# Denominators of the first token group of a linear-attention pair: a 0/1 matmul replaced by DMAs over partitions

## The chip, the cores and the metric

The kernel runs on one NeuronCore of one Trainium2 chip. The metric is the device time of one execution in microseconds, taken as the median of several runs. A run also leaves a profile: every instruction of every engine with its start and duration, and the DMAs with their landing times. TensorE (PE) does the matmuls, VectorE (DVE) and ScalarE (ACT) the elementwise work, GpSimd (POOL) and SyncE (SP) mostly issue DMAs.

## The reference

Two independent linear-attention blocks A and B, each on its own x (2048 x 640) and weights, and their outputs side by side:

```python
def block(x, wqkv, wo):                     # x 1 x 2048 x 640, H = 32 heads, Dh = 20
    q, k, v = split_heads(x @ wqkv)
    phi = lambda t: jnp.where(t > 0, t + 1, jnp.exp(t)) + 1e-6
    pq, pk = phi(q), phi(k)
    kv  = jnp.einsum("bhsd,bhse->bhde", pk, v)
    z   = jnp.einsum("bhsd->bhd", pk)
    num = jnp.einsum("bhqd,bhde->bhqe", pq, kv)
    den = jnp.einsum("bhqd,bhd->bhq", pq, z)[..., None] + 1e-6
    return merge_heads(num / den) @ wo
out = concatenate([block(A...), block(B...)], axis=-1)
```

## The kernel before, in words

All matmuls work on float32 values that are split into a rounded high part and a low remainder (names ending in h and l): ACT copies the value to the high part, VectorE subtracts it from the value to get the low part, and TensorE does three matmuls (high by high, high by low, low by high) for each product. `split` is that pair of operations; `later(1, ...)` puts the VectorE half one slot later.

There are two stages. The first works through branches A and B in eight token groups of 512 tokens: k is formed, phi(k) taken, its products with x summed into `gacc` (`psg` in PSUM), the column sums of phi(k) accumulated to DRAM by DMA (`zd`), and from these the matrix m = kv times wo is formed per branch (`kvmm`, `mmm`). m's sums and differences (`form_...`, the tiles f, fh, fl and fs) serve a product scheme of seven products instead of eight (`STEPS`, `product`, `combine`), used for k and again for the output.

The second stage goes through the eight token groups u = 0 to 7 (0 to 3 are branch A, 4 to 7 branch B). For each group `qmm` computes q in five chunks c of 128 columns, 15 matmuls each into a bank `psq`; ACT takes exp and relu from it, VectorE mixes them to phi(q) (`qphi`, line 957), and `qacc` adds z times the chunk to the accumulator `acc` (ACT for chunk 0, VectorE line 980 for the others). Group 6 (`EARLY`) is the exception: its q is computed at the very start of the kernel (`first_chunk`, `q7`, tiles w7 and x7, line 1193), stored, and loaded again late.

The columns of q are ordered by d and head, so one row of acc holds the sum over a part of the d's of one head: partition p belongs to head p mod 32, and the denominator of a head is the sum of four rows, 32 partitions apart. Two ways to form that sum stand in the code:

- group 0 only: `split_acc` splits acc into `ac`, `denmm` multiplies it by the 0/1 matrix `same` (entry 1 where two partitions belong to the same head) in two matmuls into `psd` (lines 993 and 994), and `recip` takes the reciprocal of the result, all 128 partitions by 512 columns, in two halves (line 999). `same` is made early from an iota by two VectorE operations (lines 318 and 319).
- groups 1 to 7: `spread` lays each of the four blocks of acc (32 partitions by 512 columns) over all 128 partitions, as one of four quarters of 128 columns of the tile `da` (four DMAs, line 1008); `invert` adds the quarters and takes the reciprocal of the 128 by 128 sums (lines 1014 to 1016); `gather` lays these back on each of the four blocks of `rd` (four DMAs, line 1025).

Then `divide` multiplies phi(q) by the reciprocals, in place, in two halves of 256 tokens (line 1032), `a_split` and `d_sums` with `d_split` form the left operands of the output product (da and ds, high and low parts, index 0 and 1), and `outmm(u)` does the 14 steps of the output product: seven products n = 0 to 6 for each half q of the group. Product 0 reads da 0, products 1 and 2 read ds 0; products 3 and later read da 1, and products 4 and 6 read ds 1.

The order on each engine is the program's. In the first stage it comes from positions: matmul steps are numbered, `job` places the other work at the position of a step plus a shift from the table SHIFT (and often plus fixed amounts behind the job it follows), and everything is sorted. For instance, for chunk k of the EARLY group:

```python
a = job(("ah", k), a, w7_hi, k)
job(("bh", k), a + 0.2, x7_hi, k)
job(("al", k), a + 0.4, w7_lo, k, after=[("ah", k)])
job(("bl", k), a + 0.6, x7_lo, k, after=[("bh", k)])
```

where a is the position of the first step of chunk k - 1 (for k = 4: 14; for k = 3: 8), and `job` adds and returns the shift. In the second stage work hangs on slots: ("q", i, c, k) is the slot behind the three matmuls k of chunk c of the i-th group in order, ("o", u, s) the slot behind step s of group u's output product; `at(slot, f, ...)` appends to a slot, moved by the table AT along the line of slots. The slots of group 0's output product come behind those of group 1's q. So group 0's denominators, division and splits are placed among the q matmuls of group 1. In group 0's old chain, `split_acc` is moved three slots by AT and `d_split` of index 1 too.

DMAs issued on SP go out in program order: an issue that waits for its data holds up all issues behind it. The same holds for the instructions of ACT when a DMA is issued there.

Of the kernel before, what the change touches and what calls it, by code (L numbers as in the profile page):

```python
# [7 lines left out]
F32 = mybir.dt.float32  # L8
BF16 = mybir.dt.bfloat16
F32R = mybir.dt.float32r  # L10
I32 = mybir.dt.int32
# [3 lines left out]
H = 32  # L15
DH = 20
# [10 lines left out]
    ('c5', 9): 1.08, ('counts',): 0.93, ('exp', 0): 1.45, ('exp', 1): 1.74, ('exp', 10): 0.29, ('exp', 11):  # L27
# [21 lines left out]
    23): 1.04, ('mix', 29): 2.2, ('mix', 3): 0.48, ('mix', 4): -0.12, ('mix', 5): -0.61, ('mix', 7): 1.38,  # L49
# [78 lines left out]
    ('a_split', 1, 0): 2, ('a_split', 2, 0): -1, ('a_split', 3, 0): -1, ('a_split', 4, 0): -3, ('a_split', 5,  # L128
    0): -1, ('a_split', 5, 1): -3, ('a_split', 6, 0): 5, ('a_split', 7, 1): -6, ('d_split', 0, 1): 3,
    ('d_split', 1, 1): 5, ('d_split', 2, 0): -4, ('d_split', 6, 1): 3, ('d_sums', 1, 0): 4, ('d_sums', 3, 1): 3,  # L130
    ('d_sums', 5, 0): 1, ('d_sums', 5, 1): 2, ('d_sums', 6, 1): 4, ('divide', 1, 0): 1, ('divide', 2, 0): 1,
    ('divide', 3, 0): 4, ('divide', 5, 0): 1, ('divide', 6, 0): 2, ('early_acc', 1): 6, ('early_acc', 2): 4,
    ('early_acc', 3): 10, ('early_acc', 4): 2, ('form_last', 'm', 1): 5, ('form_load', 0, 1): 3, ('form_load',
    0, 2): 9, ('form_load', 0, 9): 4, ('form_split', 'm', 1, 0): 5, ('form_split', 'm', 1, 1): -4,
    ('form_split', 'm', 1, 2): -3, ('form_split', 'm', 1, 3): -11, ('form_split', 'm', 1, 5): -4, ('form_split',
    'm', 1, 8): 3, ('form_split', 'm', 1, 9): 5, ('form_sums1', 'm', 1, 1): -5, ('gather', 1): 3, ('invert', 3):
# [14 lines left out]
def tile_linear_attn_pair(ctx: ExitStack, tc: tile.TileContext, ins, out: bass.AP):  # L151
# [153 lines left out]

    def counts():
        ij, at = base.tile([P, D], F32, name="ij", tag="kvt", bufs=1), 0
# [1354 lines left out]
```

## Time and profile before

| what | value |
|---|---|
| median of 3 runs | 560.45 us (560.14 to 561.48) |
| profiled execution: its time, its span | 560.23 us, 558.4 us |
| granted TensorE clock, mean | 0.999 |
| busy TensorE (matmul) | 553.5 us, 99% |
| busy TensorE (weight load) | 505.0 us, 90% |
| busy VectorE, ACT, POOL | 448.4, 334.6, 94.7 us |
| DMA | 116.40 MB, mean 208 GB/s |

The span is the time from the first to the last instruction of the profiled execution; the execution's own time is some 2 us longer. Busy times are unions of instruction records; a row of the profile's timeline is the start in us from the beginning of the span, the duration, the engine, the line of the kernel, the operation, the tile written and the tiles read (buffer numbers left out), and in brackets the idle time before it with what ended it. A row of the waits is who waited for whom: total us, times, longest.

### The profile page before, as it was taken

How to read it: one execution, taken by the hardware profiler on the slowest of the kernel's cores; microseconds unless marked ns; L12 is line 12 of the kernel's file. 1: busy time of each engine (PE TensorE's matmuls, PEld its weight loads, DVE VectorE, ACT ScalarE, POOL GpSimd, SP SyncE). 2: the span in 40 equal slices, each digit the busy share in tenths (PEclk: the TensorE clock that was granted, in tenths of full speed). 3: DMA queues.
4: the chain of work that ended last, by engine and by line, in shares of the span. 5: the costliest groups of instructions: out<-in, count | busy, mean ns of one | idle time of the engine just before them, and what ended most of it. 6: DMA issues, size and time to landing. Idle time of an engine off the chain costs nothing.

```text
span 558.4 us, 9225 instructions
## 1 busy us (share of the span) xinstructions
PE 553.5 (99%) x3339; PEld 505.0 (90%) x3339; DVE 448.4 (80%) x754; ACT 334.6 (60%) x607; POOL 94.7 (17%) x159
## 2 busy tenths in 40 slices
PE   9999999999999999999999999999999999999997
PEld 6898998989898999898988889989898898989997
DVE  5999869989648678797876599798888978798861
ACT  5998466775438686666673677364554646453541
POOL 0022112241101221213301120311101220010110
PEclk9999999999999999999999999999999999999999
DMA  9666577997997657697988965573726489533322
GB/s 298 243 192 140 119 215 189 282 249 232 344 329 195 176 138 210 135 280 222 274 272 250 346 223 206 161 257 100 253 82 216 157 271 382 163 120 114 114 94 95
DMA packets 58430, 116.40 MB, mean 208 GB/s; under 512 B 9104, under 2 KB 22160, under 8 KB 58256
## 3 DMA queue, kind: packets, MB, share of 16 engines
q1 hardware_dynamic: 45056, 74.58, 41.2%
q0 software_dynamic: 12784, 40.97, 26.1%
q8 instruction: 26, 0.43, 0.3%
q10 hardware_dynamic: 544, 0.26, 0.2%
q14 instruction: 20, 0.16, 0.1%
HBM read 69.82 MB, written 42.29 MB: 201 GB/s over the span
## 4 chain that ended last, share of the span: by engine, by line
PE 96%; DVE 2%; DMA 1%; issue 0%; SPq 0%; DVEq 0%
PE pa L356 25%; PE pe L356 13%; PE psg L221 8%; PE psg L220 8%; PE psg L222 8%; PE psb L356 8%; PE psq L220 7%; PE psq L222 7%; PE psq L221 7%; PE pskv L768 1%; DMA wst<-in_A_wk 1%; PE psm L220 1%; PE psq L1193 1%; PE psm L222 1%; PE psm L221 1%
## 5 line engine op out<-in xcount | busy, mean ns | idle before, releaser
L220 PE MATMUL psq<-xqh,wqh 128*128 128x512 f32 x175 | 68.4, 391 | 0.0
L222 PE MATMUL psq<-xqh,wql 128*128 128x512 f32 x175 | 68.2, 390 | 0.0
L221 PE MATMUL psq<-xql,wqh 128*128 128x512 f32 x175 | 68.1, 389 | 0.0
L220 PE MATMUL psg<-pkh,xnh 128*128 128x512 f32 x160 | 62.8, 392 | 0.0
L221 PE MATMUL psg<-pkl,xnh 128*128 128x512 f32 x160 | 62.7, 392 | 0.0
L222 PE MATMUL psg<-pkh,xnl 128*128 128x512 f32 x160 | 62.6, 391 | 0.0
L360 ACT ACTIVATE o<-pa 128x320 f32<-128x320 f32 x64 | 28.0, 438 | 54.5 <-PE pa L356 54.5
L360 ACT ACTIVATE ko<-pa 128x320 f32<-128x320 f32 x64 | 27.7, 435 | 39.7 <-PE pa L356 39.0
L568 POOL DMA_DIRECT2D zd<-ek x30 | 26.6, 886 | 119.2 <-DVE ek L560 53.9
L222 PEld LDWEIGHTS psq<-xqh,wql 128*128 128x128 f32 x175 | 32.9, 188 | 7.0
L221 PEld LDWEIGHTS psq<-xql,wqh 128*128 128x128 f32 x175 | 32.9, 188 | 6.6
L220 PEld LDWEIGHTS psq<-xqh,wqh 128*128 128x128 f32 x175 | 32.8, 188 | 6.5
L222 PEld LDWEIGHTS psg<-pkh,xnl 128*128 128x128 f32 x160 | 30.0, 188 | 6.5
L451 ACT ACTIVATE ksh<-sx 128x512 fp32r<-128x512 f32 x32 | 19.9, 633 | 26.3 <-DVE sx L469 26.2
L221 PEld LDWEIGHTS psg<-pkl,xnh 128*128 128x128 f32 x160 | 30.0, 188 | 5.4 <-DVE pkl L576 0.4
L220 PEld LDWEIGHTS psg<-pkh,xnh 128*128 128x128 f32 x160 | 30.1, 188 | 5.2
L560 DVE SCALAR_TENSOR_TENSOR ek<-ek,ko 128x640 f32<-128x640 f32 x32 | 26.3, 820 | 10.0 <-ACT ko L557 10.0
L955 ACT ACTIVATE pq<-psq 128x512 f32<-128x512 f32 x35 | 20.7, 591 | 19.6 <-PE psq L222 19.6
L572 ACT ACTIVATE pkh<-ek,epst 128x640 fp32r<-128x640 f32 x32 | 26.0, 826 | 8.8 <-DVE ek L560 8.6
L614 DVE TENSOR_TENSOR gacc<-psg,gacc 128x512 f32<-128x512 f32 (+2 forms) x42 | 25.6, 627 | 6.9 <-PE psg L222 6.9
L213 ACT ACTIVATE dah<-pq 128x1024 fp32r<-128x1024 f32 (+2 forms) x24 | 17.7, 772 | 21.9 <-DVE pq L1032 21.9
L957 DVE SCALAR_TENSOR_TENSOR pq<-pq,rq 128x512 f32<-128x512 f32 x35 | 24.0, 687 | 8.3 <-ACT rq L956 8.3
(208 smaller groups left out, 1750.7 us busy)
## 6 DMA issues: line engine op xcount, KB each, us to landing
zd<-ek POOLq DMA_DIRECT2D x32, 320.0 KB, 5.1
out<-o POOLq DMA_DIRECT2D x28, 320.0 KB, 3.5
xt<-in_A_xt_tiles SPq DMA_DIRECT2D x16, 320.0 KB, 5.5
xt<-in_B_xt_tiles SPq DMA_DIRECT2D x16, 320.0 KB, 4.1
xn<-in_B_x SPq DMA_DIRECT2D x16, 320.0 KB, 4.9
xqs<-in_A_xt SPq DMA_DIRECT2D x20, 256.0 KB, 6.6
fdmh<-fsh POOLq DMA_DIRECT2D x14, 320.0 KB, 4.0
fdml<-fsl POOLq DMA_DIRECT2D x14, 320.0 KB, 4.6
```

What stands on the lines that cost most here:

```text
L220: nc.tensor.matmul(o, whi, xhi, start=first, stop=False)
L221: nc.tensor.matmul(o, whi, xlo, start=False, stop=False)
L222: nc.tensor.matmul(o, wlo, xhi, start=False, stop=last)
L356: nc.tensor.matmul(o, x, y, start=start and m == r == 0, stop=m == len(terms) - 1 and r == 2, skip_group_check=True)
L360: nc.scalar.activation(x, y, AF.Copy)
L451: nc.scalar.activation(hi, src, AF.Copy)
L560: nc.vector.scalar_tensor_tensor(ek[n], ek[n], 1.0, rk[n], op0=OP.min, op1=OP.add)
L568: nc.gpsimd.dma_start(zacc[b], e, accum_op=OP.add)
L572: nc.scalar.activation(pk[n][0], ek[n], AF.Identity, bias=epst)
L614: nc.vector.tensor_tensor(o, x, o, op=OP.add)
L955: nc.scalar.activation(e, ps, AF.Exp)
L957: nc.vector.scalar_tensor_tensor(e, e, 1.0, r, op0=OP.min, op1=OP.add)
```

## The change

Group 0 gets its denominators like the groups 1 to 7: `spread`, `invert`, `gather`. For group 0 the eight DMAs alternate between the ACT and the SP queue; for the others all stay on SP. `split_acc`, `denmm`, `recip`, the matrix `same` and its part of the iota go. Group 0's d is formed in another order and partly in later slots: both divides in one slot, a_split before d_sums, and d_split of index 1 inside the output product. The transpose and sum of branch B's z move from group 1's q into group 0's output product. Besides that a number of entries of SHIFT, MOVED and AT change, so that jobs of the first stage, loads, splits and the chains of later groups stand in other places.

The diff, with the tables cut to the entries that are spoken of:

```diff
 SHIFT = {
-... ('ah', 4): -1.75 ... ('al', 3): 0.5 ... ('bl', 1): -0.23 ... ('bl', 3): 0.4, ('bl', 4): 3.53 ...
+... ('ah', 4): -0.43 ... ('al', 3): 1.85 ... ('bl', 1): -0.29 ... ('bl', 3): 3.06, ('bl', 4): 2.02 ...
-... ('c2', 1): 1.11 ... ('exp', 0): 1.45 ... ('mix', 5): -0.61 ... ('nl', 2): 11.78 ... ('qe', 2): -1.84 ...
+... ('c2', 1): 1.24 ... ('exp', 0): 1.24 ... ('mix', 5): 9.51 ... ('nl', 2): 13.98 ... ('qe', 2): -2.5 ...
-... ('s2', 2): 0.94 ... ('wf', 0, 1, 'l'): -0.23 ... ('xh', 3, 'A5'): -5.773 ...
+... ('s2', 2): 1.13 ... ('wf', 0, 1, 'l'): -0.42 ... ('xh', 3, 'A5'): -3.95 ...
 AT = {
+... ('a_split', 0, 0): 1 ... ('d_sums', 0, 0): 2 ... ('gather', 0): 1 ... ('spread', 0): -1 ... ('z_store', 1): -1
-... ('d_split', 0, 1): 3 ... ('split_acc', 0): 3 ... ('load_z', 1): 3 ... ('z_out', 1): 4, ('z_turn', 1): 1
+... ('load_z', 1): 9 ... ('d_sums', 1, 1): 6 ... ('d_split', 2, 1): 6 ... ('divide', 2, 0): 5 ...
...
-    same = base.tile([P, P], F32R)
...
-        nc.gpsimd.iota(mask[P], pattern=[[1, P]], base=0, channel_multiplier=-1)
...
-        ij = mask.pop(P)
-        nc.vector.tensor_scalar(ij, ij, H - 1, None, op0=OP.bitwise_and)
-        nc.vector.tensor_scalar(same, ij, 0.0, None, op0=OP.is_equal)
...
-    def split_acc(u): ...
-    def denmm(u): ...
-    def recip(u, h): ...
     def spread(u):
...
-            nc.sync.dma_start(t[0][:, j * P:(j + 1) * P], acc[u][32 * j:32 * (j + 1), :])
+            (nc.sync if u else (nc.scalar, nc.sync)[j % 2]).dma_start(t[0][:, j * P:(j + 1) * P], acc[u][32 * j:32 * (j + 1), :])
     def gather(u):
...
-            nc.sync.dma_start(r[32 * j:32 * (j + 1), :], y[:, 3 * P:])
+            (nc.sync if u else (nc.scalar, nc.sync)[j % 2]).dma_start(r[32 * j:32 * (j + 1), :], y[:, 3 * P:])
     def outmm(u):
...
-            product(n, ps[q], [da[u, i, q] for i in range(2)], [ds[u, i, q] for i in range(2)], right)
+            product(n, ps[q], [da.get((u, i, q)) for i in range(2)], [ds.get((u, i, q)) for i in range(2)], right)
...
-    at(("q", 1, 3, 3), z_turn, 1)
-    at(("q", 1, 4, 2), z_store, 1)
-    at(("q", 2, 0, 0), z_back, 1)
-    at(("q", 2, 2, 0), z_out, 1)
+    at(("o", 0, 5), z_turn, 1)
+    at(("o", 0, 6), z_store, 1)
+    at(("o", 0, 12), z_back, 1)
+    at(("q", 2, 1, 0), z_out, 1)
...
     chain = {
-        0: [(("q", 1, 0, 0), split_acc, 0), (("q", 1, 1, 1), denmm, 0), (("q", 1, 1, 1), recip, 0, 0),
-            (("q", 1, 1, 1), recip, 0, 1), (("q", 1, 1, 2), divide, 0, 0), (("q", 1, 1, 4), divide, 0, 1),
-            (("q", 1, 2, 0), d_sums, 0, 0), (("q", 1, 2, 2), a_split, 0, 0), (("q", 1, 2, 4), d_sums, 0, 1),
-            (("q", 1, 3, 1), d_split, 0, 0), (("q", 1, 3, 4), a_split, 0, 1), (("q", 1, 4, 1), d_split, 0, 1)]}
+        0: [(("q", 1, 0, 1), spread, 0), (("q", 1, 1, 2), invert, 0), (("q", 1, 1, 2), gather, 0),
+            (("q", 1, 2, 2), divide, 0, 0), (("q", 1, 2, 2), divide, 0, 1), (("q", 1, 3, 0), a_split, 0, 0),
+            (("q", 1, 3, 1), d_sums, 0, 0), (("q", 1, 4, 0), d_split, 0, 0), (("q", 1, 4, 0), a_split, 0, 1),
+            (("q", 1, 4, 1), d_sums, 0, 1), (("o", 0, 1), d_split, 0, 1)]}
```

In SHIFT and AT the position of an entry has no meaning; an entry that is not in the table counts as 0.

More of the change, by code (lines that the diff above doesn't have):

```diff
@@ L121 @@
     ('G', 2, 5): 2.0, ('G', 6, 0): 4.0, ('H', 3, 0, 0): 3.5, ('H', 7, 2, 2): 1.5, ('Q', 1, 1): 2, ('Q', 1, 2):
[3 rows of a table removed]
[3 rows of a table added]
 }
 AT = {
[L128 to L136, printed above, removed]
@@ L137 @@
-    -1, ('invert', 4): -1, ('invert', 5): -2, ('invert', 6): -4, ('kv_step', 1, 5): -2, ('load_px', 4): -1,
-    ('load_w', 'm', 1, 2): 4, ('load_w', 'm', 1, 4): -5, ('load_w', 'q', 1, 4): 8, ('load_xraw', 2, 0): 6,
-    ('load_xraw', 2, 3): 2, ('load_xraw', 4, 2): 6, ('load_xraw', 7, 0): -2, ('load_xraw', 7, 1): 2,
-    ('load_xraw', 7, 3): -6, ('load_xraw', 7, 4): 4, ('load_z', 1): 3, ('m_step', 1, 0): 2, ('m_step', 1, 2): 1,
-    ('m_step', 1, 3): 1, ('round_xq', 1, 0): -2, ('round_xq', 2, 1): -3, ('round_xq', 2, 3): -4, ('round_xq', 4,
@@ L142 @@
-    1): -4, ('round_xq', 4, 2): 2, ('round_xq', 5, 1): 1, ('round_xq', 5, 4): -3, ('round_xq', 7, 1): 4,
-    ('round_xq', 7, 4): -3, ('split_acc', 0): 3, ('split_o', 1, 1): -1, ('split_o', 1, 3): -2, ('split_w', 1,
-    0): -3, ('split_w', 1, 2): -7, ('split_w', 1, 4): 1, ('spread', 6): 6, ('z_out', 1): 4, ('z_turn', 1): 1,
+    ('a_split', 0, 0): 1, ('a_split', 1, 0): 2, ('a_split', 2, 0): -1, ('a_split', 3, 0): -1, ('a_split', 4, 0):
+    -3, ('a_split', 4, 1): 4, ('a_split', 5, 0): -1, ('a_split', 5, 1): -3, ('a_split', 6, 0): 5, ('a_split', 7,
@@ new lines @@
+    1): -6, ('d_split', 1, 1): 5, ('d_split', 2, 0): -4, ('d_split', 2, 1): 6, ('d_split', 6, 1): 3, ('d_sums',
+    0, 0): 2, ('d_sums', 1, 0): 4, ('d_sums', 1, 1): 6, ('d_sums', 3, 1): 3, ('d_sums', 4, 0): -4, ('d_sums', 5,
+    0): 1, ('d_sums', 5, 1): 2, ('d_sums', 6, 1): 4, ('divide', 1, 0): 1, ('divide', 2, 0): 5, ('divide', 3, 0):
+    4, ('divide', 5, 0): 1, ('divide', 6, 0): 2, ('early_acc', 1): 6, ('early_acc', 2): 4, ('early_acc', 3): 10,
+    ('early_acc', 4): 2, ('form_last', 'm', 1): 5, ('form_load', 0, 1): 7, ('form_load', 0, 2): 6, ('form_load',
@@ new lines @@
+    0, 6): 3, ('form_load', 0, 7): -2, ('form_load', 0, 8): -4, ('form_load', 0, 9): 5, ('form_split', 'm', 1,
[3 rows of a table added]
+    ('invert', 3): -1, ('invert', 4): -1, ('invert', 5): -2, ('invert', 6): -4, ('kv_step', 1, 5): -2,
+    ('load_px', 4): -1, ('load_w', 'm', 1, 0): -4, ('load_w', 'm', 1, 2): 3, ('load_w', 'm', 1, 4): -5,
+    ('load_w', 'q', 1, 1): -3, ('load_w', 'q', 1, 4): 8, ('load_xraw', 2, 0): 10, ('load_xraw', 2, 1): 2,
+    ('load_xraw', 2, 2): 6, ('load_xraw', 2, 3): 2, ('load_xraw', 3, 4): -2, ('load_xraw', 4, 2): 6,
@@ new lines @@
+    ('load_xraw', 7, 0): -2, ('load_xraw', 7, 1): 2, ('load_xraw', 7, 3): -6, ('load_xraw', 7, 4): 4, ('load_z',
+    1): 9, ('m_step', 1, 0): 2, ('m_step', 1, 2): 1, ('m_step', 1, 3): 1, ('round_xq', 1, 0): -5, ('round_xq',
+    1, 3): 1, ('round_xq', 2, 0): 2, ('round_xq', 2, 1): -3, ('round_xq', 2, 2): 2, ('round_xq', 4, 1): -4,
+    ('round_xq', 4, 2): 2, ('round_xq', 5, 1): 1, ('round_xq', 5, 4): -3, ('round_xq', 7, 1): 4, ('round_xq', 7,
+    4): -3, ('split_o', 1, 1): -1, ('split_o', 1, 2): -6, ('split_o', 1, 3): -5, ('split_w', 1, 0): -3,
@@ L145 @@
+    ('split_w', 1, 2): -7, ('split_w', 1, 4): 1, ('spread', 0): -1, ('spread', 6): 6, ('z_store', 1): -1,
 }
@@ L307, in counts @@
         ij, at = base.tile([P, D], F32, name="ij", tag="kvt", bufs=1), 0
-        for n in (P, 3 * DH, 2 * DH):
-            mask[n] = ij[:, at:at + n].bitcast(I32) if n == P else ij[:, at:at + n]
+        for n in (3 * DH, 2 * DH):
+            mask[n] = ij[:, at:at + n]
             at += n
-        nc.gpsimd.iota(mask[P], pattern=[[1, P]], base=0, channel_multiplier=-1)
         for nh in (3, 2):
@@ L983, in early_acc @@
         qacc(EARLY, c, px[c])
-    def split_acc(u):
-        t = q2[0].tile([P, 2, 512], F32R, name="ac", tag="sr", bufs=2)
-        split(t[:, 0], t[:, 1], acc.pop(u))
-        acc[u] = t
-    def denmm(u):
-        t = acc.pop(u)
-        ps = den.pop(u) if u in den else bank("psd")
-        nc.tensor.matmul(ps, same, t[:, 0], start=True, stop=False)
-        nc.tensor.matmul(ps, same, t[:, 1], start=False, stop=True)
-        den[u] = (ps, q2[0].tile([P, 512], F32, name="rd", tag="rd", bufs=1))
-    def recip(u, h):
-        ps, r = den[u]
-        nc.vector.reciprocal(r[:, h * 256:(h + 1) * 256], ps[:, h * 256:(h + 1) * 256])
     def spread(u):
```

4 lines of the change are left out of this document (2 added, 2 removed), and 27 rows, old and new, of tables (AT, MOVED, SHIFT).

## The prediction

> **What bounds the kernel now.** I read the page's busy shares and slices first, then the chain that ended last, then what TensorE waited for, then the timeline round the two matmuls that go.
>
> ```profile
> span 558.4 us, 9225 instructions
> PE 553.5 (99%) x3339; PEld 505.0 (90%) x3339; DVE 448.4 (80%) x754; ACT 334.6 (60%) x607; POOL 94.7 (17%) x159
> ...
> PE   9999999999999999999999999999999999999997
> ...
> PE 96%; DVE 2%; DMA 1%; issue 0%; SPq 0%; DVEq 0%
> ...
> PE psi L1137 <- PEq L1647: 0.8, 1, 0.8
> PE psq L1193 <- DVE x7l L210: 0.4, 2, 0.2
> PE psq L1231 <- ACT x7h L1217: 0.2, 1, 0.2
> ```
>
> TensorE is busy in 553.5 of 558.4 us, and 96% of the chain is its own instructions. The last three rows are the whole list of its visible waits, 1.4 us in all, and all of them belong to the preparation of the EARLY group at the start. So time moves here in two ways only: TensorE gets less work, or something arrives too late for it. The other engines' loads matter only through the second.
>
> A busy matmul record overlaps its successor, so what a matmul costs must be read from starts, not durations.
>
> ```profile
> 328.15 0.39 PE L222 MATMUL psq<-xqh,wql 128*128 128x512 f32 x1
> 328.37 0.40 PE L993 MATMUL psd<-ac,same 128*128 128x512 f32 x1
> 328.61 0.40 PE L994 MATMUL psd<-ac,same 128*128 128x512 f32 x1
> 328.84 0.40 PE L220 MATMUL psq<-xqh,wqh 128*128 128x512 f32 x1
> ```
>
> Rows are start, duration, engine, line, tiles. Neighbours start 0.22 to 0.24 us apart though each lasts 0.40.
>
> **The change part by part.**
>
> *The two denominator matmuls.* From the first one's start to the start of the matmul behind them, 328.84 - 328.37 = 0.47 us leave a TensorE that has no visible wait there. Ends: 0.44 us (twice the neighbours' shortest spacing, 328.37 - 328.15 = 0.22) and 0.79 us (both durations, as if nothing overlapped). I take 0.47, the starts being what the successor feels. The Trainium skill, page "TensorE: Matmul & The Clock Gate", section "Wait — 56ns, not 53.3ns?", says a warm matmul of 512 columns starts 215.7 ns after the last. By it the pair would be worth an estimated 0.43 us and the sum below 0.04 us smaller; this case's starts, 0.23 to 0.24 us apart, are slightly longer, and they decide.
>
> *A swap at the start.* Among the changed entries of SHIFT are those of chunk 4 of the EARLY group. Position of a job = position of its step plus its shifts. Before: w7_hi sits at 14 - 1.75 = 12.25, so w7_lo at 12.25 + 0.4 + 2.31 = 14.96 and x7_lo at 12.25 + 0.6 + 3.53 = 16.38. After: w7_hi at 14 - 0.43 = 13.57, w7_lo at 13.57 + 0.4 + 2.31 = 16.28, x7_lo at 13.57 + 0.6 + 2.02 = 16.19. VectorE thus does x7l first. For chunk 3 the two move later (10.2 and 10.3 become 11.55 and 12.96), but no other VectorE job lies between 7.78 and 13.66, so that order stays and its wait stays.
>
> ```profile
> 18.38 0.82 DVE L210 TENSOR_TENSOR w7l<-w,w7h 128x640 fp32r<-128x640 f32 x1
> 19.12 0.69 DVE L210 TENSOR_TENSOR x7l<-x,x7h 128x512 fp32r<-128x512 f32 x1
> 19.72 0.42 DVE L469 TENSOR_TENSOR sx<-xt 128x256 f32<-128x256 f32 x1
> ...
> 19.26 0.39 PE L1193 MATMUL psq<-x7h,w7h 128*128 128x512 f32 x1
> 19.86 0.50 PE L1193 MATMUL psq<-x7l,w7h 128*128 128x512 f32 x1 [0.21 <-DVE x7l L210]
> 20.20 0.40 PE L1193 MATMUL psq<-x7h,w7l 128*128 128x512 f32 x1
> ```
>
> x7l (0.60 us to its successor) would run at 18.38 and w7l at 18.98, done at 18.98 + 0.82 = 19.80. The matmul on x7l can start unhindered at 19.26 + 0.23 = 19.49; that on w7l follows w7l's end by 0.05 us (as 19.86 follows 19.12 + 0.69 = 19.81), at 19.85 instead of 20.20. Gain 0.35 us; late next is w7l, by 0.85 - 0.72 = 0.13. Ends: nothing (something downstream eats it) and 0.48 (20.20 - 19.26 less two spacings of 0.23). I take 0.35.
>
> *First group's denominators by DMAs.* Removed: ACT copy and VectorE difference of ac, two reciprocals. Added: four DMAs out (each lays 32 partitions by 512 columns over 128 by 128), two adds and one reciprocal, four DMAs back, half of them issued by ACT. Seven groups already do this, so their rows price it.
>
> ```profile
> L1008 SPq DMA_DIRECT2D da<-acc x28: 594/606/1229, 348.4 to 512.1; - x28
> L1014 DVE TENSOR_TENSOR da<-da x7: 415/416/427, 354.2 to 514.4; 128x256 f32<-128x256 f32 x7
> L1015 DVE TENSOR_TENSOR da<-da x7: 291/293/293, 354.7 to 514.9; 128x128 f32<-128x128 f32 x7
> L1016 DVE RECIPROCAL da<-da x7: 953/953/954, 355.0 to 515.2; 128x128 f32<-128x128 f32 x7
> ...
> DMA to landing us min/median/max: 2.1/2.2/5.5
> ...
> 0.75 0.41 ACTq L1155 DMA_DIRECT2D x<-in_B_xt_tiles  x1
> ...
> 324.53 0.75 DVE L980 SCALAR_TENSOR_TENSOR acc<-pq,z,acc 128x512 f32<-128x512 f32 x1
> 328.33 0.69 DVE L957 SCALAR_TENSOR_TENSOR pq<-pq,rq 128x512 f32<-128x512 f32 x1 [0.38 <-ACT rq L956]
> 329.04 3.37 DVE L999 RECIPROCAL rd<-psd 128x256 f32<-128x256 f32 x2
> 332.33 2.82 DVE L1032 SCALAR_TENSOR_TENSOR pq<-pq,rd 128x1280 f32<-128x1280 f32 x2
> 341.51 1.22 DVE L210 TENSOR_TENSOR dsl<-sr,dsh 128x1024 fp32r<-128x1024 f32 x1
> 342.65 0.84 DVE L699 STREAM_TRANSPOSE zt<-zs 128x640 f32<-128x640 f32 x1
> 343.52 0.82 DVE L701 TENSOR_REDUCE zr<-zt 128x20 f32<-128x640 f32 x1
> ...
> 343.07 1.76 PE pa L356 x12
> 344.84 1.76 PE pe L356 x12
> ```
>
> (The rows of a tile give ns min/median/max; the last two are from the chain, the first group's output product, whose pe part is the first to need dsl.) In before's clock: acc is done at 324.53 + 0.75 = 325.28. ACT and SP issue two DMAs each, 0.41 to 0.61 us apiece; the last starts at 325.95 and lands 2.2 later, 328.2. The program puts invert behind chunk 0's mix and the second m_step's slot; an ACT delayed by its two issues lets that mix end about 329.4, so invert finds its data there and takes 0.42 + 0.29 + 0.95 = 1.66: 331.1. Back: last issue 331.75, landing 333.95. The divides stand in slot (q,1,2,2) behind chunk 1's mix and accumulation, which end about 334.4 (ACT waits for the reciprocal, issues until 332.05, and then needs about 1.0 for chunk 1's exp and relu; the mix and the accumulation take 0.69 and 0.75, starting 0.6 to 0.7 apart): 334.4 to 337.25, against 332.33 to 335.15 now. The order behind them is a_split 0 (its difference done by 339.7), d_sums 0 (341.0), chunk 3's mix and accumulation (342.3), then dsl: 342.3 + 1.2 = 343.5, against 342.73 now. TensorE, 0.47 us earlier, starts the pe part at 344.37 and reads dsl by its third matmul (12 in 1.76, so 0.15 apart), 344.66. So dsl comes later by 0.8 us and still has 1.2 us; dal (needed at 342.9) has 3. These ends are estimates from the rows above; bounds for the stall follow as rivals. I take nothing. d_split 1 moves into the output product, where the first product to read it is step 8 of 14; I estimate about 2 us left there.
>
> *What is queued behind the new waits.* On SP the spread waits for acc at 325.28; behind it stand the last loads of the forms, wanted from the fourth product on, about 348; from 326.6 they have over 20 us. On ACT, behind the spread, stand two copies of wo and chunk 0's exp and relu, about 1 us late; a bank of psq is wanted again only four allocations on. Behind the gather stands chunk 1's exp, late by about 0.5.
>
> *z of branch B* (transpose and sum, 0.84 + 0.82) moves from before the output product into it: VectorE is relieved in just the stretch that it is full. Group 4 is the first to read z. Nothing.
>
> *The 0/1 matrix* (one iota, two VectorE operations), *mix 5 ten positions later* (with its z store, rounding and difference; first consumer at position 68, it lands near 59), *the other shifts, and the d parts of later groups in other slots*: none belongs to a visible TensorE wait.
>
> ```profile
> 20.00:40.00 20.00, 20.00 (x128) 19.20 (x129) 19.62 (x41) 19.40 (x41) 3.09 (x5) 1.00 0.49 173
> 40.00:100.00 60.00, 60.00 (x345) 55.14 (x344) 52.79 (x106) 38.78 (x69) 11.80 (x18) 1.00 0.69 169
> ```
>
> (Window, us; busy PE, PEld, DVE, ACT, POOL; clock; DMA share.) What hides them is that TensorE has no idle time from 20 us on. Thin cover is 20 to 40, where VectorE and ACT are at 98 and 97%: from -0.1 to +0.35, the latter the whole start gain. I take 0.
>
> **Sum.** -0.47 - 0.35 = -0.82 us. The profiled execution took 560.23 us with a span of 558.4, so a span of 557.6; it stood 0.22 under the median 560.45, and the prediction is 560.45 - 0.82 = 559.6.
>
> **The rivals.**
>
> *Late landings (slower).* The small DMAs do not always land in 2.2 us. The first of the present gathers:
>
> ```profile
> L1025 SPq DMA_DIRECT2D rd<-da x4: 604/628/1240, 356.0 to 358.0; - x4
> DMA to landing us min/median/max: 5.5/5.5/5.5
> ...
> 358.00:360.00 2.00, 2.00 (x13) 1.78 (x12) 1.18 (x3) 0.46 (x1) 1.59 (x4) 1.00 1.02 367
> ...
> 320.00:325.00 5.00, 5.00 (x28) 4.41 (x27) 4.93 (x8) 4.85 (x11) 0.66 (x2) 1.00 1.01 384
> 325.00:328.00 3.00, 3.00 (x15) 2.49 (x14) 2.95 (x5) 2.49 (x5) 1.68 (x3) 1.00 0.74 243
> 331.00:334.00 3.00, 3.00 (x16) 2.45 (x15) 3.00 (x3) 1.13 (x3) 1.16 (x2) 1.00 0.81 213
> ```
>
> Those 5.5 us fell where the DMA engines were full, and the new hops fall at 0.74 and 0.81 of full. If both hops take 5.5: the spread lands at 331.45, invert starts 2.0 late, the gather lands at 333.75 + 5.5 = 339.25, the divides are 4.85 late, TensorE stalls 4.85 - 1.2 = 3.65: 563.3. It counts as slower from a lateness of 3.7 us on (the 1.2, the 0.82 and 0.3%, which is 1.7 us and about what a measurement here can tell from no change). Against it: the loads that fill 320 to 325 are now partly held behind the spread, and at least half of the present hops out landed in 2.1 to 2.2 (minimum and median of da's row above). *Only the gather late:* 2.85 late, stall 1.65, 561.3, no change. The Trainium skill, page "DMA: Bandwidth & Descriptors", section "Issuing engines are not separate DMA queues", speaks for these two: all issuers share the same 16 DMA engines, and a second issuer saves issue time alone. By that rule the half issued by ACT would land no earlier among the loads; no row before shows small DMAs from ACT in such company.
>
> *Only the matmuls count:* the 0.35 is eaten in 20 to 40 us: 560.0.
>
> *More goes at the start (faster):* the pair is worth 0.79 and both x7l waits go (0.48 each): 558.7. Against it: starts, not durations, and chunk 3's order does not change.
>
> **How the numbers follow.** Forecast 0.62, only the matmuls 0.14, gather late 0.12, both late 0.06, more at the start 0.06. Faster takes the last, slower the late pair with a little for a stall elsewhere: 0.06, 0.87, 0.07. The range takes the first three with the spread of the runs round the lowest: 558.9 to 561.3.
>
> **What would show it.** No psd rows; TensorE starts at 0.22 to 0.24 us right through 328; near 19.9 us the wait changes to w7l and shrinks, near 16.9 it stays; da<-acc and rd<-da on two queues near 326 and 331, landing in 2.2 to 3; dsl done a little under 344.4 with no wait of TensorE on it. A visible wait on dsl or dah near 344, or on ko, kal or ksl between 25 and 45, makes it wrong.

## The result, and the profile after

| | median of 6 runs | profiled execution | its span |
|---|---|---|---|
| before | 560.32 us (560.14 to 561.48) | 560.23 us | 558.4 us |
| after | 564.1 us (563.51 to 564.61) | 564.1 us | 562.3 us |

The change makes the kernel slower: ratio 1.0065, 95% interval 1.0052 to 1.0078. The forecast was 559.6 us and its range ended at 561.3; it was wrong. The row of TensorE's busy slices on the page of the changed kernel, and the new rows in the list of TensorE's waits (who waited for whom, total us, times, longest):

```profile
PE   9999999999999999999999998999999999999997
```

```profile
PE pe L355 <- DVE dsl L214: 0.9, 1, 0.9
PE pa L355 <- ACT o L359: 0.8, 1, 0.8
...
PE pa L355 <- DVE dal L214: 0.8, 1, 0.8
PE pe L355 <- ACT dsh L217: 0.7, 1, 0.7
```

One slice of TensorE's row fell from 9 to 8, and four waits are new: three for the halves of the first group's left operands (dal, dsh, dsl), one for a bank that ACT has not copied out (pa). The matmuls that waited lie within 14 us; here is the last of them, counted from start to start as in the prediction's first step:

```profile
356.12 0.31 PE L355 MATMUL pa<-f,dal 128*128 128x320 f32 x1
357.24 0.56 PE L355 MATMUL pa<-f,dah 128*128 128x320 f32 x2 [0.81 <-ACT o L359]
357.64 0.31 PE L355 MATMUL pa<-f,dal 128*128 128x320 f32 x1
```

From 356.12 to 357.24 are 1.12 us where neighbours start 0.15 apart, 0.97 lost, and the pair behind it needs 0.40 instead of 0.29. The four stops cost 4.2 us in this way, 3.1 of them the three for the left operands and 1.1 the one for pa. With the 0.47 us of the two matmuls and a second stage that begins 0.19 us later than before (a matmul of q at 314.80 that was at 314.61), 4.2 - 0.47 + 0.19 = 3.9 us, the difference of the two spans.

Where the operands were late shows in the timeline of the other engines (start, duration, engine, line, tiles; in brackets idle time and what ended it):

```profile
324.54 2.35 POOL L854 DMA_DIRECT2D md<-mev  x4 [4.21 <-ACT mev L359]
...
324.87 1.32 ACTq L991 DMA_DIRECT2D da<-acc  x2
...
324.91 1.61 SPq L991 DMA_DIRECT2D da<-acc  x2
326.61 0.55 SPq L930 DMA_DIRECT2D fh<-fdmh  x1
...
332.36 0.42 DVE L997 TENSOR_TENSOR da<-da 128x256 f32<-128x256 f32 x1 [3.00 <-DMA da<-acc]
...
332.35 0.82 ACT L977 ACTIVATE acc<-pq,zs,z 128x512 f32<-128x512 f32 x1 [3.72 <-DMA da<-acc]
...
335.82 0.60 ACT L954 ACTIVATE pq<-psq 128x512 f32<-128x512 f32 x1 [2.01 <-issue]
...
338.33 2.88 DVE L1015 SCALAR_TENSOR_TENSOR pq<-pq,rd 128x1280 f32<-128x1280 f32 x2
...
344.71 0.32 SPq L254 DMA_DIRECT2D wst<-md  x1
...
349.88 0.33 SPq L287 DMA_DIRECT2D xqs<-in_A_xt  x1
...
356.24 0.63 ACT L291 ACTIVATE xqh<-xqs 128x512 fp32r<-128x512 f32 x1 [3.96 <-DMA xqs<-in_A_xt]
```

The spread is issued from 324.87 on; VectorE, which stands waiting for it, can add the quarters only at 332.36, 7.5 us later. The forecast had 328.2 for the landing, with acc done at 325.28 where it is done at 324.83 here. Beside the spread run four stores of m by GpSimd (150 KB each, issued from 324.54) and, behind it on SP, four form loads (320 KB each). The kernel before issues the same four stores at the same time, with no spread beside them:

```profile
324.34 2.34 POOL L855 DMA_DIRECT2D md<-mev  x4 [5.16 <-ACT mev L360]
```

In the changed kernel the divides start at 338.33 where the forecast had 334.4, and everything behind them is late. The pa wait is another chain: ACT stands 3.96 us for a chunk of x (xqs) that SP issued only at 349.88, and the copies of pa stand behind it on ACT.

At the start the swap took place: the wait on x7l near 19.86 us is gone and one of 0.15 us on w7l stands in its place (matmuls at 19.86 and 20.24), and chunk 3's stays (0.23 at 17.24).

### The profile page after: what moved, and what is told of

Its sections match the earlier page's. It is cut to its first block, busy times and chain, and to the rows that moved or that the text cites. A ratio compares the mean times of both kernels' runs of the same rounds, so it can differ in the third digit from the quotient of the medians.

```text
span 562.3 us, 9237 instructions
## 1 busy us (share of the span) xinstructions
PE 554.7 (99%) x3337; PEld 505.0 (90%) x3337; DVE 446.0 (79%) x752; ACT 332.8 (59%) x606; POOL 94.7 (17%) x158
## 5 line engine op out<-in xcount | busy, mean ns | idle before, releaser
L450 ACT ACTIVATE ksh<-sx 128x512 fp32r<-128x512 f32 x32 | 19.9, 633 | 26.8 <-DVE sx L468 26.8
L355 PE MATMUL pa<-wfh,kah 128*128 128x320 f32 x96 | 29.8, 310 | 0.0
```

Of the source, the lines that this page charges most:

```text
L355: nc.tensor.matmul(o, x, y, start=start and m == r == 0, stop=m == len(terms) - 1 and r == 2, skip_group_check=True)
L450: nc.scalar.activation(hi, src, AF.Copy)
```

## The experiments

Each but one is an edit of the changed kernel. The ratio is that to the kernel before on the same chip.

**Without the first group's denominators**

```diff
-        0: [(("q", 1, 0, 1), spread, 0), (("q", 1, 1, 2), invert, 0), (("q", 1, 1, 2), gather, 0),
-            (("q", 1, 2, 2), divide, 0, 0), (("q", 1, 2, 2), divide, 0, 1), (("q", 1, 3, 0), a_split, 0, 0),
+        0: [(("q", 1, 3, 0), a_split, 0, 0),
```

> The changed kernel with group 0's denominators left out: no spread, no invert, no gather and no divide, so group 0's output is not divided; all else as changed. If the whole loss comes from the chain of the hops: no wait near 344 to 357, and 0.47 us less than before from the matmuls plus what the start gives (0.19 by the run with the shifts alone): 559.7 to 560.0. If other parts of the diff cost something too (z inside the output product, the d parts of later groups, the later load of x): 560.5 or more, with TensorE's waits naming it.

559.56 us, ratio 0.999 [0.9982, 0.9999], and no wait of TensorE behind 20 us. So without the chain spread, invert, gather, divide there is no loss; all else in the diff together, the dropped matmuls among it, gives what the forecast's sum had. The edit also takes the chain's work off VectorE and ACT, so it shows where the loss lies, and not yet that the landing is its cause.

**The start alone** (the kernel before with the new SHIFT table)

> The kernel before with only the table SHIFT of the changed one (the swap of w7_lo and x7_lo of chunk 4, mix 5 later and the other entries of the first stage); denominators by matmuls as before. The forecast's term: 0.35 us gained at 20 us, 560.0. Rival (eaten between 20 and 40 us, or at the start): 560.3. Slower than 560.6: the other shifts cost something.

560.32 us against 560.51, ratio 0.9996 [0.9987, 1.0004]: the swap's 0.35 us can't be seen in the times; the interval allows -0.7 to +0.2 us. The traces do show a gain. From chunk 3's late matmul to the first matmul behind chunk 4's late pair the kernel before takes 20.43 - 16.86 = 3.57 us, this one 20.58 - 17.24 = 3.34 and the changed kernel 20.57 - 17.24 = 3.33: some 0.24 us less.

**The form loads in front of the spread**

```diff
+AT.update({('form_load', 0, 4): -2, ('form_load', 0, 5): -5})
```

> The changed kernel with the form loads 4 and 5 (four DMAs, 1.3 MB) issued on SP before the spread instead of right behind it. Theory A (these loads, issued from 326.6 us on, share the DMA engines with the spread and make it land after 6.7 us instead of 2.2): the spread lands near 328 to 329, invert starts near 329.5 instead of 332.4, TensorE's waits on dal, dsh and dsl (0.92 + 0.84 + 1.03 us of lost starts) go, time 560.0 to 561.2 (the upper end if the wait behind xqs stays). Rival B (the small DMAs land late by themselves, beside the m stores of GpSimd): landing stays at 6 to 7 us, time 563.5 to 564.5. Rival C (the hold on ACT by the accumulator's only buffer is what costs): as A if the landing is early, as B if not; the next run tells it apart.

562.39 us, 1.0034 [1.0022, 1.0046]: 1.7 us of the loss come back. GpSimd's stores are now the only company, and the spread is still late:

```profile
324.34 2.34 POOL L856 DMA_DIRECT2D md<-mev  x4 [4.21 <-ACT mev L361]
...
324.67 1.32 ACTq L993 DMA_DIRECT2D da<-acc  x2
...
330.64 0.42 DVE L999 TENSOR_TENSOR da<-da 128x256 f32<-128x256 f32 x1 [1.49 <-DMA da<-acc]
```

From the first issue to the add 5.97 us, and VectorE waits 1.49 us of them.

**An own buffer for the first group's acc.** acc has one buffer, so ACT's first sum for the next group can't be written before the spread has read the old one (the 3.72 us above).

```diff
+            if u == 0:
+                acc[u] = q2[0].tile([P, 2, 512], F32, name="ac0", tag="sr", bufs=2)[:, 0]
```

> The changed kernel with group 0's accumulator in a buffer of its own (one of the two of tag sr), so that ACT's first accumulation of group 1 need not wait until the spread has read it. Theory A: the spread still lands at about 332.3 us and invert still starts at 332.4; ACT takes chunk 1's exp at its time, the divides start about 1.5 us earlier (336.8 instead of 338.3), half of the 2.8 us of lost starts on dal, dsh and dsl stays: 562 to 563. Rival C (the hold on ACT is the cost): all of them go, 560.3 to 561.3. Rival D (the hold costs nothing beside the landing): 564.1, no change.

564.29 us, 1.0057 [1.0039, 1.0075]: no gain that shows. The six executions scatter from 561.9 to 565.4 us, and three of them, like three of the changed kernel's, had a lowered mean clock (0.997, see the last section), so a gain of some tenths can't be excluded. The sum is no longer held, and ACT waits at the next place instead, behind the gather's issue (333.55 to 335.13), which needs the late reciprocal; PE, which the bracket names, had been done long before:

```profile
329.53 0.81 ACT L979 ACTIVATE acc<-pq,zs,z 128x512 f32<-128x512 f32 x1 [0.76 <-DVE pq L956]
335.17 0.60 ACT L954 ACTIVATE pq<-psq 128x512 f32<-128x512 f32 x1 [4.18 <-PE psm L226]
```

**The x load at its old place**

```diff
+AT.update({('load_xraw', 2, 0): 6})
```

> The changed kernel with one table entry taken back: the load of chunk 0 of x for the third group ten slots later becomes six again. If its slot is why ACT sits on xqh until 356.2 us and TensorE loses 1.08 us behind it (pa not copied out): that wait goes, 563.0, the three waits near 344 to 348 stay. If SP, held until 344.7 by the store of m, is why: chunk 0 still arrives after 353 and the time stays at 563.8 to 564.1.

563.56 us, 1.0058 [1.0043, 1.0072]. In its trace the pa wait is gone and the three others stay:

```profile
PE pe L357 <- DVE dsl L216: 0.9, 1, 0.9
...
PE pa L357 <- DVE dal L216: 0.8, 1, 0.8
PE pe L357 <- ACT dsh L219: 0.7, 1, 0.7
```

The time fell by 0.5 us against the changed kernel, with intervals that overlap; alone it shows where the pa wait comes from, not what it is worth.

**All eight DMAs on SP**

```diff
-            (nc.sync if u else (nc.scalar, nc.sync)[j % 2]).dma_start(...)
+            nc.sync.dma_start(...)
```

> The changed kernel with all eight small DMAs of group 0 on SP, as the other groups have them. If a second issuer saves only issue time: the hops land about as late (the loads behind the spread start 1.2 us later, the gather's last issue 1.2 us later), ACT is no longer held by the gather, chunk 1's mix goes ahead of it; the divides start at 338 to 339 as now: 563.8 to 564.6. If ACT's being held by these issues is the cost: the divides start before 337 and the time falls under 563.

562.63 us, 1.0052 [1.0036, 1.0068]. ACT is no longer held by the issues, but now the divides wait for the gather:

```profile
338.21 2.90 DVE L1015 SCALAR_TENSOR_TENSOR pq<-pq,rd 128x1280 f32<-128x1280 f32 x2 [2.65 <-DMA rd<-da]
```

They start at 338.21, as in the changed kernel (338.33): the hold on ACT and the landing of the gather stand beside each other, and taking one away bares the other. The three waits stay. Yet the time is 1.5 us lower by the medians (the intervals overlap), under the 563 that was expected only if the divides came earlier. What went is the fourth wait, the one for pa: ACT copies m's last rows without standing behind the gather, so m's last two stores start at 335.35 instead of 337.83, the load that waits for them is issued at 339.53 instead of 344.71, and the chunk of x behind it at 346.52 instead of 349.88.

**Stores behind, first try** (loads in front, and the slots of m's stores 2 and 3 moved behind the gather, still on GpSimd)

```diff
-        at((... ("q", 1, 0, 1), ("q", 1, 0, 3), ("q", 1, 1, 4) ...)[g], store_m, nc.gpsimd, g)
+        at((... ("q", 1, 1, 4), ("q", 1, 1, 4), ("q", 1, 1, 4) ...)[g], store_m, nc.gpsimd, g)
```

> The changed kernel with form loads 4 and 5 issued before the spread, and the stores of m groups 2 and 3 (four DMAs of 150 KB on GpSimd, which start with the spread at 324.5 us) moved behind the invert's slot. Theory A (the spread lands late because of whatever other transfers run beside it; with the loads away it still had the stores beside it and landed at 330.6): it lands at 328 or a little after, invert starts near 329.5 without an idle wait of more than 0.5 us, the waits on dsh and dsl go or stay under 0.3 us together; 560.0 to 560.6, with up to 0.4 of it the wait behind xqs. Rival B (the small DMAs take 5 us here whatever runs beside them): lands at 330.5 again, 562.2 to 562.6.

562.04 us, 1.0032 [1.002, 1.0044], the same as with the loads moved alone. The edit did nothing: GpSimd has little to do, runs ahead of the slots and issues a store as soon as its data is there (four at 323.79 in this trace). A slot orders the work of one engine; it does not hold a transfer back on an idle one.

**The same with an own acc buffer and the x load back**

> As the quiet spread (form loads 4 and 5 before it, stores of m 2 and 3 behind the invert), and group 0's accumulator in a buffer of its own, and the load of x chunk 0 for the third group back at six slots. Theory A with the sum of the forecast: none of the four waits near 344 to 357 is left, the two matmuls are saved: 559.6 to 560.2, a little under the kernel before. Rival (the chain is too long for its place even with 2.2 us hops): a wait on dsl of 0.5 to 1 us stays, 560.5 to 561.

561.75 us, 1.0023 [1.0014, 1.0032]: a little better, with the wait on dsl still 0.9 us and the stores still beside the spread. The loss is not in these two.

**Stores really behind** (loads in front; SP issues stores 2 and 3, behind the gather)

```diff
-           store_m, nc.gpsimd, g)
+           store_m, nc.sync if g in (2, 3) else nc.gpsimd, g)
```

> The changed kernel with the two form loads in front of the first group's spread, and now really with m's third and fourth row group stored behind the gather: SyncE issues those four stores, where GpSimd issued them just ahead of the spread. Nothing but the spread's own 0.26 MB is then under way when it starts (acc's last sum ends near 324.6). Theory A (the landing is late because of the company): the spread lands near 328 to 328.5 instead of 330.6, the inverse starts near 329.5, the difference dsl ends some 2 us earlier than in the kernel with only the loads moved, the waits of TensorE of 1.02, 0.33 and 0.43 us on dsl, dsh and the pa copy mostly go: 560.5 or less. Theory B (eight small DMAs over two queues need some 5 us by themselves): the spread still lands at 330 or later, the waits stay, 562.2.

560.7 us, 1.0007 [0.9998, 1.0016]; the waits on dal, dsh and dsl are gone. The rows, and one of the table by stretches (us; busy PE, PEld, DVE, ACT, POOL; clock, DMA share, GB/s):

```profile
324.26 1.32 ACTq L993 DMA_DIRECT2D da<-acc  x2
...
328.67 0.42 DVE L999 TENSOR_TENSOR da<-da 128x256 f32<-128x256 f32 x1
```

```profile
328.00:330.00 2.00, 2.00 (x13) 1.77 (x12) 1.89 (x5) 1.24 (x4) 0.00 (x0) 1.00 0.00 0
```

No transfer runs between 328 and 330, so the spread had landed by 328.0, 3.0 us at most behind its last issue (at 325.0). The add at 328.67 follows other work of VectorE without idle time. What is left is the pa wait (0.9), which was expected to go too.

**The same with an own acc buffer and the x load back**

> The kernel with the loads in front and the two stores behind, and besides it an own buffer for the first group's acc (so that ACT's first sum of the next group does not wait until the spread has read it) and the load of the next x chunk at its old place. Theory A: all four causes of the hop chain's lateness but the gather's issue on ACT are gone, no wait of TensorE behind 20 us, 559.7 to 560.2. Theory B: like the kernel with stores behind alone, about 562.

560.22 us, 0.9999 [0.999, 1.0008], and no wait of over 0.3 us is left in the second stage.

**And the gather on SP**

> The same with all four DMAs of the gather on SyncE (the spread still alternates between ACT and SyncE), so that chunk 1's exp on ACT does not stand behind an issue that waits for the reciprocal. If that hold still matters (VectorE idle some 2.8 us in front of chunk 1's mix in the kernel with the loads in front), the divides start about 1 us earlier relative to the reciprocal or wait for rd alone, and the time is at or below that of the kernel before it, 559.6 to 560.0; if the gather's landing is what the divides wait for, issuing it with one engine is 1.2 us later and a wait on dsl of up to 0.5 us remains: 560.3.

561.07 us, 1.0013 [1.0004, 1.0023], 0.85 us above the kernel with two issuers. Chunk 1's mix comes earlier (332.36 instead of 333.90), but VectorE then stands 1.13 us before the divides for rd. Neither expectation held whole. Counted from the spread's first issue the divides start after 10.5 us (334.96 - 324.42), with two issuers after 10.8 (335.30 - 324.55), so the gather on one engine made nothing later there, and no wait on dsl is in the list of TensorE's waits. The longest in its second stage are 0.3 us each, for xql and for a sum of the output (o), elsewhere; where the 0.85 us come from stays open.

**Stores behind, loads left beside** (the store edit alone)

> The changed kernel with the third and fourth of m's stores behind the gather, but the two form loads (four DMAs, 1.28 MB) left where the change has them, right behind the spread on SyncE: the cell that is still missing beside both companies (564.1), stores alone (562.39) and neither (560.7). If each company delays the landing on its own, the spread lands between 329.5 and 331.5, one TensorE wait of some 0.5 to 1 us on dsl and one on pa's copy remain, 561.5 to 562.5. If SyncE's half of the spread, being ahead of the loads in the queue, is not delayed and the stores were the cause, it lands near 328.5 and the time is 560.7 or less. If the loads alone are the cause, it lands at 332 and the time is 564.

560.55 us, 1.0005 [0.9996, 1.0014]. This was not what I expected: each company delaying on its own would have given 561.5 to 562.5. The profiled execution (which started its second stage some 1.7 us late, so only differences are read) has

```profile
326.20 1.33 ACTq L991 DMA_DIRECT2D da<-acc  x2
...
327.89 0.55 SPq L930 DMA_DIRECT2D fh<-fdmh  x1
...
330.61 0.42 DVE L997 TENSOR_TENSOR da<-da 128x256 f32<-128x256 f32 x1
```

4.41 us from first issue to the add, again with no idle time before it, although 1.28 MB of loads follow the spread on SP. Loads behind the spread are harmless by themselves; the stores are not; and with the stores there the loads add 1.5 us (7.5 against 5.97).

**Stores from SP, right behind the spread** (loads in front)

```diff
-        at((... ("q", 1, 0, 1), ("q", 1, 0, 3), ("q", 1, 1, 4) ...)[g], store_m, nc.gpsimd, g)
+        at((... ("q", 1, 0, 1), ("q", 1, 0, 1), ("q", 1, 1, 4) ...)[g], store_m, nc.sync if g in (2, 3) else nc.gpsimd, g)
```

> The kernel with the two form loads in front of the spread, and m's third and fourth row group (four DMAs, 0.6 MB) issued by SyncE right behind its half of the spread instead of by GpSimd at the same moment: the same bytes start some 1.6 us later and from SyncE. If the amount of data beside the spread decides, the spread lands near 330.5 and the time is 562.4, as with GpSimd's stores. If it decides that the stores come from GpSimd's queue or stand ahead of the spread, the spread lands by 328.7, no wait on dsl of over 0.3 us remains, 560.3 to 561.

560.17 us, 0.9995 [0.9986, 1.0004]. The same 0.6 MB, issued from SP and from 1.6 us later on, don't delay the spread:

```profile
324.35 1.32 ACTq L993 DMA_DIRECT2D da<-acc  x2
...
326.04 3.30 SPq L856 DMA_DIRECT2D md<-mev  x4
...
328.76 0.42 DVE L999 TENSOR_TENSOR da<-da 128x256 f32<-128x256 f32 x1
```

A wait of 0.4 us on dsl is left, a little more than I allowed. For the two DMAs of the spread on SP the traces also give the landing itself. Counted from their own issue, first with SP's stores behind them, then with GpSimd's stores beside them (the run with the form loads in front):

```profile
DMA to landing us min/median/max: 2.5/2.5/2.6
```

```profile
DMA to landing us min/median/max: 3.8/4.5/5.1
```

So these bytes near the spread are harmless when they come from SP and behind it. Who issues them, that they start before it, or how many of them are under way is left: when the spread landed, near 327.6, SP had issued two of its four stores (326.04 and 326.98). The Trainium skill, page "DMA: Bandwidth & Descriptors", section "SWDGE vs HWDGE vs iDMA", says that GpSimd's transfers and those of SP and ACT sit in different queues of each DMA engine, between which the engine goes round in turn. The trace agrees in so far as SP's half of the spread lands in 2.5 to 2.6 us with SP's stores behind it, and in 3.8 to 5.1 us with GpSimd's stores beside it.

**Issuer or place?** Three kernels with the whole spread on ACT (2.6 to 3.1 us of issuing), loads in front, and the four stores from GpSimd at the same moment, from SP at the same moment, or from SP behind the gather.

```diff
-            (nc.sync if u else (nc.scalar, nc.sync)[j % 2]).dma_start(t[0]...)
+            (nc.sync if u else nc.scalar).dma_start(t[0]...)
```

> Base for two others: the kernel with the form loads in front of the spread, and all four DMAs of the first group's spread on ACT, so that the spread shares no issuing queue with m's stores. The stores of m's third and fourth row group come from GpSimd at the moment of the spread, as the change has them. ACT needs some 2.6 us to issue, so the landing without company would be 1.3 us later than with two issuers. If GpSimd's stores delay the spread whatever queue it uses, the inverse starts 6 us or more behind the first issue; if only SyncE's half was delayed, some 4.5 to 5 us behind it.

> The same, but SyncE issues the four stores (0.6 MB), from the same moment on as ACT issues the spread. If what matters is that the stores are ahead of or beside the spread, whoever issues them, the inverse starts as late as with GpSimd's stores (6 us or more behind the first issue of the spread). If it matters that GpSimd issues them, it starts some 5 us behind it, as without stores.

> The same with the four stores on SyncE behind the gather: nothing beside the spread. The inverse starts 4.4 to 5 us behind the first issue of the spread (4.4 us with two issuers, where VectorE's work in front of it set the start and not the landing).

563.63 us (1.0058 [1.0025, 1.0092]), 562.44 (1.0033 [1.0022, 1.0044]) and 562.47 (1.0038 [1.0025, 1.005]). With GpSimd's stores:

```profile
326.04 3.06 ACTq L993 DMA_DIRECT2D da<-acc  x4
...
332.39 0.81 ACT L979 ACTIVATE acc<-pq,zs,z 128x512 f32<-128x512 f32 x1 [0.85 <-DMA da<-acc]
...
DMA to landing us min/median/max: 4.2/4.4/4.7
```

and with SP's, issued from 323.81 on:

```profile
324.40 2.76 ACTq L993 DMA_DIRECT2D da<-acc  x4
...
330.36 0.82 ACT L979 ACTIVATE acc<-pq,zs,z 128x512 f32<-128x512 f32 x1 [0.76 <-DVE pq L958]
...
DMA to landing us min/median/max: 2.5/2.7/3.0
...
327.42 0.72 SPq L856 DMA_DIRECT2D md<-mev  x1
```

ACT's sum, which overwrites acc, starts 6.35 us behind the first issue with GpSimd's stores and is released by the DMA; with SP's stores it is 5.96 us and released by VectorE, the landing having come earlier; the quiet control has 5.82, again released by VectorE. The inverse starts 6.36 us behind the first issue, 5.84 and, in the control, 5.70; the expectations for the last two (some 5, and 4.4 to 5) were missed, because VectorE's mix in front of it comes late when ACT issues all four DMAs. The landing itself is plainer. The last row of the first fence, and the last but one of the second, give it for the third and fourth DMA of the spread, from their own issue: 4.2 to 4.7 us with GpSimd's stores, 2.5 to 3.0 with SP's, where the present hops out of the other groups have a median of 2.2. In time, too, SP's stores cost nothing that shows beside the control.

That is not yet the issuer alone. GpSimd issues its four stores within 1.8 us (325.71 to 327.47), all of them before the spread's last DMA (328.10). SP issues two, and its third only at 327.42 and its fourth at 328.50, when the spread's last DMA (326.54) was under way or about to land. So twice the bytes ran beside the spread in GpSimd's case, and whether the issuer or that amount decides was not tried apart. On either reading it is GpSimd's four stores, as the change has them, that make the spread late: by 1.6 us or more between 5.97 (stores by GpSimd) and 4.41 (by SP, set by VectorE) of the kernels above.

**The smallest repair** (stores behind; the x load and its rounding where the kernel before has them; loads left beside the spread)

```diff
+AT.update({('load_xraw', 2, 0): 6, ('round_xq', 2, 0): 0})
...
-           store_m, nc.gpsimd, g)
+           store_m, nc.sync if g in (2, 3) else nc.gpsimd, g)
```

> The changed kernel with two edits only: the two stores behind the gather, and the load of group 2's first x chunk and its rounding at the places that the kernel before has for them. If the stores and that load are all that the change lost, TensorE has no wait behind 20 us of over 0.3 us: 559.8 to 560.2, at or just below the kernel before. If the loads behind the spread cost something after all, a wait on dsl of 0.5 us or more shows: 560.7 or more.

559.49 us, ratio 0.9984 [0.9975, 0.9993]: faster than before by 0.9 us, and than the changed kernel by 4.6. All three visible waits of TensorE are at the start again, and the first hop lands in time:

```profile
PE psi L1122 <- PEq L1632: 0.8, 1, 0.8
PE psq L1216 <- ACT x7h L1202: 0.4, 1, 0.4
PE psq L1178 <- DVE x7l L216: 0.2, 1, 0.2
```

```profile
324.51 1.32 ACTq L993 DMA_DIRECT2D da<-acc  x2
...
328.91 0.42 DVE L999 TENSOR_TENSOR da<-da 128x256 f32<-128x256 f32 x1
...
335.08 2.89 DVE L1017 SCALAR_TENSOR_TENSOR pq<-pq,rd 128x1280 f32<-128x1280 f32 x2 [0.19 <-DMA rd<-da]
...
343.13 1.22 DVE L216 TENSOR_TENSOR dsl<-sr,dsh 128x1024 fp32r<-128x1024 f32 x1
```

dsl is done at 343.13 + 1.22 = 344.35, and TensorE takes it at once:

```profile
344.15 0.31 PE L357 MATMUL pe<-fl,dsh 128*128 128x320 f32 x1
344.41 0.41 PE L357 MATMUL pe<-fh,dsl 128*128 128x320 f32 x1
344.66 0.31 PE L357 MATMUL pe<-fh,dsh 128*128 128x320 f32 x1
```

The third matmul of the pe part starts 0.26 us behind its neighbour instead of 0.15, and the next one 0.25: the slack is used up, and 0.1 to 0.2 us beyond it. The landings of the spread in one table, from its first issue to the first work that reads it (where the reader did not wait, the landing was earlier than that):

| company of the spread | us | the reader waited for it | time, us |
|---|---|---|---|
| stores by GpSimd and loads (the change) | 7.5 | yes | 564.1 |
| stores by GpSimd | 5.97 | yes | 562.39 |
| stores by SP, right behind | 4.41 | no | 560.17 |
| loads | 4.41 | no | 560.55 |
| loads, and the x load back | 4.40 | no | 559.49 |
| none | 4.41 | no | 560.7 |

## Why the prediction was wrong, step by step

- *The two denominator matmuls*, 0.47 us: right. From the start of the q matmuls at 324.29 to that of the m matmuls (psm) behind them are 5.24 us before (to 329.53) and 4.77 after (324.48 to 329.25). Without the chain's lateness the kernel is at 559.56 (denominators left out) and 559.49 (repaired), and the forecast was 559.6.
- *A swap at the start*, 0.35 us: the swap and its new wait on w7l (0.15; forecast 0.13) came as worked out, chunk 3's wait stayed as worked out. Its worth was 0.24 us in the traces, less than the 0.35, because the matmul behind the new wait also starts 0.1 us late (0.33 behind the waiting one instead of 0.23). In the times it is not shown: 0.2 us by the medians of the experiment, with an interval round nothing, and the profiled execution of after had lost more than that earlier, with data that arrived later at 8 to 12 us.
- *First group's denominators by DMAs*, "I take nothing": this is the step that failed, and the term in it is the landing, 2.2 us from the last issue. It was 7.5 us from the first issue, some 6.7 from the last. With quiet DMA queues it is 3.0 or less. The hops out that gave the 2.2 landed in 2.1 to 3.3 us, all of them in the later groups. The second hop was sized too short as well: in the repaired kernel the divides start 335.08 - 330.67 = 4.4 us behind the gather's first issue, with VectorE waiting for rd, and the forecast had landed it 2.85 behind (331.1 to 333.95). Counted from acc's end (324.48 there, 325.28 in the forecast) dsl is done after 19.9 us where the forecast had 18.2, and TensorE wants it after 19.8 instead of 19.4. So the margin of 1.2 us was gone even in good company, with a stall of 0.2 us at most; anything that came on top of it was lost time.
- The rival *Late landings* had half of the mechanism and nearly the right time (563.3), and got 0.06. The spread was late, as it says, and later than its 5.5 us. The gather was not: it had landed when the divides started at 338.33, 3.5 us behind its last issue (334.8), and they followed chunk 1's accumulation without idle time. Of the 4.2 us lost, 1.1 came from the x load, which the rival does not have, so that its time came out near is partly luck. The sentence against it ("the loads that fill 320 to 325 are now partly held behind the spread") looked at the wrong transfers: the loads behind the spread do no harm by themselves, as the experiment with them alone shows. What was under way at the spread's start were m's stores, which GpSimd issues as soon as their data is there; the prediction priced neither their bytes nor their queue, though the kernel before issues them at the same time (324.34). I weighed the share of busy DMA (0.74) instead of asking which transfers start beside the new ones and who issues them.
- The Trainium skill, page "DMA: Bandwidth & Descriptors", section "Issuing engines are not separate DMA queues" (all issuers share the engines, a second issuer saves issue time alone), was weighed as to ACT's half of the spread. The traces agree that a second issuer saves little: with the gather on two engines the divides start 10.8 us behind the spread's first issue, on one 10.5.
- *What is queued behind the new waits*: I looked for who is late on SP and ACT, and found slack of 20 us for the loads, which held. I missed that acc has one buffer, so that ACT's next sum waits for the landing too; the experiment with an own buffer shows no gain clear of its scatter. The hold of chunk 1's exp behind the gather's issue was counted (the 334.4 for the divides rests on it), but with the reciprocal in time: a late first hop is handed on whole through ACT to the mix that stands before the divides, whatever the second hop does.
- *The other shifts*, taken as 0 because none belonged to a visible wait: ('load_xraw', 2, 0) from 6 to 10 was one that mattered. At 10 the x chunk is issued behind two loads of which one waits for m's last store; that store is late because ACT copies m's last rows only behind the gather's issue, and so the entry became the pa wait of 0.8 to 1 us. With either taken away, the entry or the hold on ACT (all eight DMAs on SP), the wait is gone. Moving it and its rounding back is worth 1.1 us where the stores are out of the way (560.55 to 559.49).
- *z of branch B, the 0/1 matrix, mix 5*: nothing that shows, as taken; no wait of the repaired kernel names them.

## What to carry to other kernels

A hop through DMA on a critical path is as long as its company lets it be: before giving it the median landing, list the transfers that start beside it on every queue, those of an idle engine above all, which here issued as soon as its data was there wherever its slot stood. Then follow the hop's lateness through each engine in order, the one that issues the next hop included, to the first consumer with no slack; where that slack is 1.2 us, a landing of 6 instead of 2 is the whole result. And when a table of places is retuned along with an edit, each entry that moves a load behind one that can wait is a term of its own.

## What the runs showed of the hardware that I had not expected

- Four stores of 0.6 MB by GpSimd beside it delay a spread of 0.26 MB in 512-byte pieces by at least 1.6 us: its DMAs landed 3.8 to 5.1 us after their issue. With the same stores by SP, behind the spread or from the same moment on, they landed in 2.5 to 3.0. SP had then only two of the four stores under way, so issuer and amount are not told apart.
- GpSimd, with little else to do, issued its stores when their data was there: with their calls moved behind the gather they still started at 323.79, beside the spread.
- Short stops were followed by half the matmul clock. In two profiled executions, of the kernel with all eight DMAs on SP and of that with the own acc buffer, TensorE's waits of 0.3 to 0.9 us between 342 and 348 were followed by a stretch at 0.50. The first kernel's rows behind the last stop, and that of the changed kernel, which has the same waits and kept its clock:

```profile
348.00:350.00 2.00, 2.00 (x9) 2.00 (x9) 2.00 (x5) 0.78 (x4) 0.00 (x0) 0.50 1.01 380
350.00:352.00 2.00, 2.00 (x13) 2.00 (x12) 1.96 (x3) 1.78 (x3) 0.00 (x0) 0.74 0.25 87
```

```profile
348.00:350.00 2.00, 2.00 (x16) 2.00 (x15) 2.00 (x5) 0.83 (x3) 0.00 (x0) 1.00 0.85 194
```

Nine matmul records lie in those 2 us where the other has 16. With TensorE busy throughout I estimate the cost at 2 x 0.50 + 2 x 0.26 = 1.5 us from the first two rows, beside waits of 2.2 us in all. It came in some executions and not in others. A mean clock of 0.997 or less, which is what such a stretch makes of 560 us, stands in 3 of 6 executions of the changed kernel, 3 of 6 with the own acc buffer, 2 of 6 with all eight DMAs on SP and 1 of 6 with the x load back. These are the four kernels whose traces have all three stops on dal, dsh and dsl; every execution of the others is at 0.999 or more. Why it comes in some executions alone wasn't tried. The Trainium skill, page "TensorE: Matmul & The Clock Gate", section "HAM oscillation — how this bites in real kernels", gives as the abstract rule no idle gap over about 3.4 us; here none was over 1.1 us and the clock still fell to 0.50, so for stops in a row the measurement decides.
